# Token-major product of attention with k times v, with the norm's statistics on 8 columns, in an attention and double-MLP kernel

## The chip, the cores and the metric

The kernel runs on one core of a Trainium2 chip. The metric is the time of one execution on the device in microseconds (us). TensorE (PE in the profile; PEld is its loading of stationary operands) multiplies matrices and writes to the accumulator memory PSUM, of which a core has 8 banks of 512 columns in 32-bit floats; VectorE (DVE) and ScalarE (ACT) read and write PSUM and the on-chip memory SBUF; GpSimd (POOL) and SyncE (SP) issue transfers (DMA) to and from main memory.

## The reference

Linear attention without softmax, a root-mean-square norm, and two MLPs, all in 32-bit floats. There are 8 batches, 8 heads, 576 tokens of each batch and 64 columns of each head, so 4608 tokens and 512 columns after the heads are laid side by side; the MLPs have 2048 hidden columns.

```python
kv = einsum('bhsd,bhse->bhde', k, v)
out = einsum('bhsd,bhde->bhse', q, kv)
rms = sqrt(mean(out * out, axis=-1, keepdims=True) + 1e-06)
x = (out / rms * g_norm)            # then (batch, token) by (head, column)
h = x @ moe_w_in;   x = (moe_s * relu(h) ** 2 + moe_b) @ moe_w_out
h = x @ moe2_w_in;  x = (h * cos(h)) @ moe2_w_out
```

## The kernel before

Tokens go in 9 blocks of 512 (`TB`). The first three blocks pass the first MLP step by step, 48 steps, 16 for each block and each for one hidden tile of 128 columns (`mm_h`, lines 654 to 671, and `mm_o`, lines 704 to 730); the other six wait in main memory (`x1_d`) and pass it later in *pairs* of hidden tiles (`mm_h2`, `mm_o1`), in which seven products take the place of eight; then all tokens pass the second MLP in the same pairs. An operand of full precision is kept as two parts, a rounded one and the remainder (`fp32r`), and a product is three matmuls of such parts. Where `f32` operands are multiplied directly, a matmul appears as two instructions.

Attention is cut into *units* (`attn_unit`, line 566): one block and one pair of heads `hp`, 128 columns. There are 9 x 4 = 36 units. The units of block 0 run at the start of the kernel (`native`); those of block 1 beside the first steps, those of blocks 2 to 8 beside steps 16 to 40. A block of 512 tokens and a batch of 576 don't fit: in blocks 1 to 7 the border of two batches lies 64, 128, 192, 256, 320, 384 and 448 tokens into the block, and the block has two *segments* with a matrix kv of their own (`segments`, line 467).

A unit does this. The matrix kv of two heads is made by 64-column products (line 542) and copied into the diagonal of `kvf` (line 552). The query tile `qT`, 128 columns of two heads by 512 tokens, comes from four transpositions on TensorE in block 0 (line 579) and from a VectorE transpose of 32 x 32 blocks later (line 599). The product (line 610) has kv as the stationary operand and the tokens moving, one matmul for each segment, so the result `xps` has the heads' columns on the partitions and 512 tokens along the columns. ScalarE squares it (line 613) and, after block 0, copies it into `qT` (line 617) so that the bank comes free. The mean of squares over the 64 columns of a head, which lie on partitions, is a product with the matrix `ones` that holds 1/64 in two diagonal squares (line 619; after block 0 in two rounded parts made at lines 623 and 624, then lines 628 and 629); the result stands on every partition of the head. From it ScalarE takes the reciprocal root and its square (lines 634, 636), VectorE refines the root by one Newton step and scales the product by it and by -g (lines 638 to 643). For the first three blocks `split_x` (line 558) makes the two parts; for the others the tile is stored to `x1_d` (line 648).

The order of every engine's instructions is worked out beforehand by a planner (class `Plan`): each `op` names its engine, an assumed cost in us, a due time, what it writes and reads, and a `margin` that its readers and the next user of its buffer keep. The planner places operations by their earliest start and due time, and hands out buffers of a pool (`t`: 6 tiles of 512 columns; `qT`: 2; `qh` and `ql`: one each; the banks `a0` to `a3`, `h0` to `h3`) to whichever comes next. After block 0, attention has the banks h2 and h3 for its kv products, its products and its mean of squares. Each engine executes its list strictly in this order. Stores go through SP's queue; a buffer that is stored is free for its next writer once the store has landed. Lines 945 to 950 are 40 filler matmuls on the identity, which the planner puts where TensorE would have nothing else.

The tiles `qT`, `qh`, `ql`, `kvf`, the query and kv loads and the identity `ident` lie in a pool `early`, whose room a pool `late` takes over in the stage of the pairs.

Of the kernel before, what the change touches and what calls it, by code (L numbers as in the profile page):

```python
# [10 lines left out]
F32 = mybir.dt.float32  # L11
F32R = mybir.dt.float32r
I32 = mybir.dt.int32
U32 = mybir.dt.uint32
AF = mybir.ActivationFunctionType
ALU = mybir.AluOpType

P = 128
TB = 512
# [4 lines left out]
NE = 3  # L24
# [19 lines left out]
LATE_BY, SLIP = 2.0, 1.5  # L44
# [124 lines left out]
def fused_kernel(  # L169
# [14 lines left out]
    nc = tc.nc  # L184
    B, H, S, D = q.shape
    NT, DM = out.shape
    DFF = moe_w_in.shape[1]
    KC = DM // P
# [10 lines left out]
    EPS = 1e-6  # L199

    cpool = ctx.enter_context(tc.tile_pool(name="cpool", bufs=1))
# [15 lines left out]
    def f32(ap):  # L217
        return ap.bitcast(F32)
# [28 lines left out]
    def pref(slots):  # L247
        return Ref(slots, lambda s: psum.tile([P, TB], F32, tag=s, name=s))

    def slots(name, n, start=0):  # L250
        return [f"{name}{i}" for i in range(start, start + n)]

    WO, WI, RAW = slots("wo", NF), slots("wi", NF), ["raw"]
    T, C = slots("t", 6), slots("c", 5)
    K_RAW, V_RAW, Q_RAW = ["kv_raw"], ["raw"], ["q_raw", "q_raw1"]
    KV_F = slots("kvf", KC)
    QT, QH, QL = ["qT", "qT1"], ["qh"], ["ql"]
# [14 lines left out]
    ACC, HB0, HB1, HB2, HB3 = slots("a", 4), ["h0"], ["h1"], ["h2"], ["h3"]  # L272


    ones = cpool.tile([P, P], F32R, name="ones")
    nc.vector.memset(f32(ones), 0.0)
    for j in range(2):

        nc.vector.memset(f32(ones)[j * D:(j + 1) * D, j * D:(j + 1) * D], 1.0 / D)
    kv_f, kv_ref = {}, {}  # L280
    for n in range(KC):
        z, u = divmod(n, 2)
# [272 lines left out]

    xs = {}

    def split_x(j, c, t, by):
        x = xs[j, c] = sref(X[c], F32R, (2, TB))
        op("ACT", 0.62, by, lambda: nc.scalar.copy(x.t[:, 0], t.t), w=[x], r=[t])  # L560
        op("DVE", 0.69, by, lambda: nc.vector.tensor_tensor(
            out=x.t[:, 1], in0=t.t, in1=f32(x.t[:, 0]), op=ALU.subtract), w=[x], r=[t])

    ms_ops, x_ops = [], []

    def attn_unit(j, hp, by, after=()):

        native = j == 0
        segs = segments(j)
        for off, n, b, s in segs:  # L570
            if s == 0 and (j == 0 or hp % 2 == 0):
                kv_unit(j, b, [hp] if j == 0 else [hp, hp + 1], by - 9, after)
        qT = sref(QT + QH + QL if native else QT)
        if j == 0:
            ps = pref([ACC[0], *HB2])

            def transpose():
                for c in range(KC):
                    nc.tensor.transpose(
                        ps.t[:, c * P:(c + 1) * P], q0[hp].t[:, 0, c, :], ident  # L580
                    )

            op("PE", 0.45, by - 11, transpose, w=[ps], r=[q0[hp]])
            op("ACT", 0.48, by - 10, lambda: nc.scalar.copy(qT.t, ps.t), w=[qT], r=[ps])
        else:
            raw = sref(Q_RAW)

            def load(off, n, b, s, z):
                h, d0 = 2 * hp + z // 2, 32 * (z % 2)
                (nc.gpsimd if j > 1 and z > 5 else nc.sync).dma_start(  # L590
                    out=raw.t.rearrange("p (c d) -> p c d", d=32)[32 * z:32 * z + 32, off // 32:(off + n) // 32, :],
                    in_=q[b, h, s:s + n, d0:d0 + 32].rearrange("(c t) d -> t c d", t=32),
                )

            for seg in segs:
                for z in range(4):
                    op(*(("SUM", 1.0) if j > 1 and z > 5 else ("SP", 0.5)), by - 17, lambda seg=seg, z=z: load(*seg, z),
                       p=[raw], after=after, margin=LATE_BY)
            op("DVE", 0.6, by - 11, lambda: nc.vector.transpose(out=qT.t, in_=raw.t), w=[qT], r=[raw], margin=SLIP,
               after=x_ops[-1:])  # L600
        kvs = [kv_f[b % 2, hp // 2] for off, n, b, s in segs]
        kv_refs = [kv_ref[b % 2, hp] for off, n, b, s in segs]
        xps = pref([*ACC[1:3], *HB3] if j == 0 else HB2 + HB3)
        sq = sref(T)
        ms = pref(ACC[3:] if j == 0 else HB2 + HB3)

        def mm_x():
            for (off, n, b, s), kvt in zip(segs, kvs):
                sl = slice(off, off + n)
                nc.tensor.matmul(xps.t[:, sl], kvt.t[:, hp % 2], qT.t[:, sl], start=True, stop=True)  # L610

        x_ops.append(op("PE", 0.9, by - 8, mm_x, w=[xps], r=[qT, *kv_refs], keep=kvs))
        op("ACT", 0.48, by - 7, lambda: nc.scalar.activation(sq.t, xps.t, AF.Square), w=[sq], r=[xps])
        x = xps
        if not native:
            x = qT
            op("ACT", 0.48, by - 7, lambda: nc.scalar.copy(qT.t, xps.t), w=[qT], r=[xps], margin=SLIP)
        if native:
            op("PE", 0.9, by - 6, lambda: nc.tensor.matmul(
                ms.t, f32(ones), sq.t, start=True, stop=True), w=[ms], r=[sq])  # L620
        else:
            sqh, sql = sref(QH, F32R), sref(QL, F32R)
            op("ACT", 0.52, by - 7, lambda: nc.scalar.copy(sqh.t, sq.t), w=[sqh], r=[sq], keep=[sql], margin=SLIP / 2)
            op("DVE", 0.6, by - 6, lambda: nc.vector.tensor_tensor(
                out=sql.t, in0=sq.t, in1=f32(sqh.t), op=ALU.subtract), w=[sql], r=[sq, sqh], margin=SLIP)

            def mm_s():
                nc.tensor.matmul(ms.t, ones, sqh.t, start=True, stop=False)  # L628
                nc.tensor.matmul(ms.t, ones, sql.t, start=False, stop=True)

            ms_ops.append(op("PE", 0.45, by - 5, mm_s, w=[ms], r=[sqh, sql]))

        r0, a = sref(T), sref(T)
        op("ACT", 0.48, by - 4, lambda: nc.scalar.activation(r0.t, ms.t, AF.Abs_reciprocal_sqrt, bias=EPS),
           w=[r0], r=[ms])
        op("ACT", 0.52, by - 3, lambda: nc.scalar.activation(a.t, r0.t, AF.Square, scale=math.sqrt(0.5)),
           w=[a], r=[r0])
        op("DVE", 0.66, by - 2, lambda: nc.vector.scalar_tensor_tensor(
            out=a.t, in0=ms.t, scalar=EPS, in1=a.t, op0=ALU.add, op1=ALU.mult), w=[a], r=[ms],
           margin=SLIP if j else 0)  # L640
        op("DVE", 0.6, by - 2, lambda: nc.vector.scalar_tensor_tensor(
            out=r0.t, in0=a.t, scalar=-1.5, in1=r0.t, op0=ALU.add, op1=ALU.mult), w=[r0], r=[a])
        op("DVE", 0.66, by - 1, lambda: nc.vector.scalar_tensor_tensor(
            out=a.t, in0=x.t, scalar=g_neg, in1=r0.t, op0=ALU.mult, op1=ALU.mult), w=[a], r=[x, r0, g_ref])
        if j < NE:
            split_x(j, hp, a, by)
        else:
            op("SP", 0.8, by, lambda: nc.sync.dma_start(out=x1_d[hp][:, j * TB:(j + 1) * TB], in_=a.t),
               w=[x1_ref[j, hp]], r=[a])

# [419 lines left out]
```

## Time and profile before

| | |
|---|---|
| median of 3 runs | 1633.51 us (1630.72 to 1633.92) |
| the profiled execution | 1634.23 us |
| its span in the profile | 1632.4 us |
| its mean granted TensorE clock | 0.999 |
| instructions | 23647 |
| PE busy | 1613.6 us, 8672 matmuls |
| DVE busy | 1137.3 us, 1796 instructions |
| ACT busy | 932.4 us, 1571 instructions |
| POOL busy | 58.6 us |

The span runs from the first to the last instruction of the program, and the execution takes 1.8 us more than its span. Busy time is what an engine's own records cover. Matmuls are pipelined and the ends of one overlap the next, so a busy PE does not mean a PE at its peak. The profile names an instruction by its line, and a tile by its pool's name without the number: `t` is any of t0 to t5, `h` any of h0 to h3, and `x_d` is `x1_d` or `x2_d`.

### The profile page before, as it was taken

How to read it: one execution, taken by the hardware profiler on the slowest of the kernel's cores; microseconds unless marked ns; L12 is line 12 of the kernel's file. 1: busy time of each engine (PE TensorE's matmuls, PEld its weight loads, DVE VectorE, ACT ScalarE, POOL GpSimd, SP SyncE). 2: the span in 40 equal slices, each digit the busy share in tenths (PEclk: the TensorE clock that was granted, in tenths of full speed). 3: DMA queues.
4: the chain of work that ended last, by engine and by line, in shares of the span. 5: the costliest groups of instructions: out<-in, count | busy, mean ns of one | idle time of the engine just before them, and what ended most of it. 6: DMA issues, size and time to landing. Idle time of an engine off the chain costs nothing.

```text
span 1632.4 us, 23647 instructions
## 1 busy us (share of the span) xinstructions
PE 1613.6 (99%) x8672; PEld 1422.6 (87%) x8672; DVE 1137.3 (70%) x1796; ACT 932.4 (57%) x1571; POOL 58.6 (4%) x94
## 2 busy tenths in 40 slices
PE   8999999999999999999999999999999999999998
PEld 6678887779999999999999989989899898998997
DVE  6887887785776756767667767667667668668564
ACT  6897765555555555555556555545546546446443
POOL 1131121000000000000000000000000000000000
PEclk9999999999999999999999999999999999999999
DMA  9965688826666747757756435444444534544431
GB/s 305 262 191 129 172 204 233 215 76 203 226 207 221 250 155 245 252 181 246 245 182 228 159 121 163 154 123 144 161 133 131 172 117 137 163 128 136 148 116 46
DMA packets 202419, 288.88 MB, mean 177 GB/s; under 512 B 87744, under 2 KB 132800, under 8 KB 202304
## 3 DMA queue, kind: packets, MB, share of 16 engines
q1 hardware_dynamic: 195376, 266.40, 52.8%
q0 software_dynamic: 6400, 20.45, 4.3%
q8 instruction: 69, 1.13, 0.3%
q10 hardware_dynamic: 528, 0.52, 0.1%
q14 instruction: 46, 0.38, 0.1%
HBM read 228.59 MB, written 58.72 MB: 176 GB/s over the span
## 4 chain that ended last, share of the span: by engine, by line
PE 94%; DMA 3%; DVE 1%; ACT 1%; issue 0%; SPq 0%; DVEq 0%; ACTq 0%
PE h L862 36%; PE a L719 22%; PE a L757 11%; PE h L719 8%; PE h L757 5%; PE h L662 2%; PE h L664 2%; PE h L663 2%; PE a L711 2%; PE h L610 1%; DMA w1i_d<-t 1%; PE h L542 1%; DMA wo<-in_v_dram 1%; PE h L628 0%; DMA w2i_d<-t 0%
## 5 line engine op out<-in xcount | busy, mean ns | idle before, releaser
L862 PE MATMUL h<-shared,wi 128*128 128x384 f32 x2208 | 459.0, 337 | 2.2 <-ACT t L874 2.2
L862 PEld LDWEIGHTS h<-shared,wi 128*128 128x128 f32 x2208 | 391.3, 188 | 16.4 <-ACT t L874 2.6
L719 PE MATMUL a<-wo,wi 128*128 128x512 f32 x964 | 258.6, 391 | 0.0
L874 ACT COPY t<-h 128x384 f32<-128x384 f32 x235 | 112.3, 478 | 198.5 <-PE h L862 180.3
L719 PEld LDWEIGHTS a<-wo,wi 128*128 128x128 f32 x964 | 180.0, 188 | 33.6
L757 PE MATMUL a<-wi,wo 128*128 128x256 f32 (+1 forms) x1152 | 203.7, 317 | 0.0
L757 PEld LDWEIGHTS a<-wi,wo 128*128 128x128 f32 x1152 | 178.7, 188 | 18.0
L719 PE MATMUL h<-wo,wi 128*128 128x512 f32 x482 | 130.1, 392 | 0.0
L916 ACT ACTIVATE wi<-wi 128x768 f32<-128x768 f32 x96 | 81.4, 848 | 76.7 <-DVE wi L914 76.7
L862 PE MATMUL h<-g,wi 128*128 128x384 f32 x552 | 123.0, 337 | 0.0
L862 PE MATMUL h<-late,wi 128*128 128x384 f32 x528 | 118.6, 335 | 0.0
L719 PE MATMUL a<-g,wo 128*128 128x512 f32 x456 | 116.5, 395 | 0.0
L908 ACT ACTIVATE wi<-wi 128x768 f32<-128x768 f32 x95 | 80.5, 848 | 47.0 <-DVE wi L878 44.9
L719 PEld LDWEIGHTS h<-wo,wi 128*128 128x128 f32 x482 | 89.8, 188 | 16.0
L757 PE MATMUL h<-wi,wo 128*128 128x512 f32 x384 | 100.7, 394 | 0.8 <-DVE wi L937 0.8
L719 PEld LDWEIGHTS a<-g,wo 128*128 128x128 f32 x456 | 84.7, 188 | 18.2
L862 PEld LDWEIGHTS h<-late,wi 128*128 128x128 f32 x528 | 94.7, 188 | 5.3
L862 PEld LDWEIGHTS h<-g,wi 128*128 128x128 f32 x552 | 97.2, 188 | 2.0 <-ACT t L874 0.2
L878 DVE TENSOR_TENSOR wi<-h,t 128x384 f32<-128x384 f32 x113 | 62.8, 556 | 48.6 <-PE h L862 35.0
L912 DVE SCALAR_TENSOR_TENSOR wi<-wi,wi 128x768 f32<-128x768 f32 x95 | 90.7, 955 | 1.7
L918 DVE TENSOR_TENSOR wi<-wi,wi 128x768 f32<-128x768 f32 x95 | 90.6, 954 | 1.4
L874 ACT COPY c<-h 128x384 f32<-128x384 f32 x85 | 40.7, 479 | 88.2 <-PE h L862 88.0
(190 smaller groups left out, 2528.4 us busy)
## 6 DMA issues: line engine op xcount, KB each, us to landing
wi<-w2i_d SPq DMA_DIRECT2D x144, 512.0 KB, 4.3
wi<-w1i_d SPq DMA_DIRECT2D x96, 512.0 KB, 4.7
late<-x_d SPq DMA_DIRECT2D x36, 384.0 KB, 5.9
wo<-in_moe_w_out_dram SPq DMA_DIRECT2D x24, 512.0 KB, 6.9
w2i_d<-t SPq DMA_DIRECT2D x48, 256.0 KB, 5.4
wi<-w2i_d SPq DMA_DIRECT2D x48, 256.0 KB, 2.7
x_d<-t SPq DMA_DIRECT2D x40, 256.0 KB, 2.6
w1i_d<-t SPq DMA_DIRECT2D x32, 256.0 KB, 3.9
```

The lines of the kernel that those rows point to most:

```text
L662: nc.tensor.matmul(h.t, wh, hi, start=(c == 0), stop=False)
L663: nc.tensor.matmul(h.t, wh, lo, start=False, stop=False)
L664: nc.tensor.matmul(h.t, wl, hi, start=False, stop=(c == KC - 1))
L719: nc.tensor.matmul(o.t, a, b, start=(first and z == 0), stop=(last and z == 2))
L757: nc.tensor.matmul(dst, x[:, sl], y[:, src], start=(first and z == i == 0), stop=(last and z == 2), skip_group_check=a >= 4)
L862: nc.tensor.matmul(o.t[:, 0:HT], a, b, start=(first and c == z == 0), stop=(c == 1 and z == 2), skip_group_check=not first)
L874: op("ACT", 0.52, by + 1, lambda: nc.scalar.copy(dst(), o.t[:, 0:HT]), p=[s], r=[o])
L878: op("DVE", 0.57, by + 1, lambda: nc.vector.tensor_tensor(out=h[f].t[:, half * HT:(half + 1) * HT], in0=a.t[:, 0:HT], in1=s.t, op=ALU.add) ...
L908: op("ACT", act, by, lambda u=u, x=x: nc.scalar.activation(u.t, x.t, AF.Identity, scale=1.0 / TWO_PI, bias=0.25), w=[u], r=[x])
L912: op("DVE", one, by + 2, lambda u=u, x=x: nc.vector.scalar_tensor_tensor(out=u.t, in0=x.t, scalar=1.0 / TWO_PI, in1=u.t, op0=ALU.mult, op1 ...
L916: op("ACT", act, by + 4, lambda u=u: nc.scalar.activation(u.t, u.t, AF.Sin, scale=TWO_PI, bias=0.5 * math.pi), w=[u])
L918: op("DVE", one, by + 5, lambda u=u, x=x: nc.vector.tensor_tensor(out=u.t, in0=u.t, in1=x.t, op=ALU.mult), w=[u], r=[x])
```

## The change

The product of a unit is turned round. The 128 tokens of a chunk are now the stationary operand and kv moves, so the result has the tokens on the partitions and, for each of four chunks, 128 columns of two heads. Where the border of two batches cuts a chunk, the chunk is done in two matmuls with 64 stationary columns each. The sum of squares runs along columns (one VectorE reduction to 8 columns: 4 chunks of 2 heads), the root and its refinement work on tiles of 8 columns (`norm`), the product is scaled by it with a broadcast, and four transpositions on TensorE turn the scaled tile back to columns on the partitions, into a bank `back`. ScalarE and VectorE read it from there with the scale -g. The matrix `ones`, the copy of the product into `qT`, the two parts of the squares and the two matmuls on them go; block 0 loses its full-precision product with `ones`. The scaled tile takes `qh` or `ql` after block 0, a tile of `t` in it.

```diff
@@ -251,7 +251,7 @@
         return [f"{name}{i}" for i in range(start, start + n)]
 
     WO, WI, RAW = slots("wo", NF), slots("wi", NF), ["raw"]
-    T, C = slots("t", 6), slots("c", 5)
+    T, C, NORM = slots("t", 6), slots("c", 5), slots("n", 4)
     K_RAW, V_RAW, Q_RAW = ["kv_raw"], ["raw"], ["q_raw", "q_raw1"]
     KV_F = slots("kvf", KC)
     QT, QH, QL = ["qT", "qT1"], ["qh"], ["ql"]
@@ -272,11 +272,6 @@
     ACC, HB0, HB1, HB2, HB3 = slots("a", 4), ["h0"], ["h1"], ["h2"], ["h3"]
 
 
-    ones = cpool.tile([P, P], F32R, name="ones")
-    nc.vector.memset(f32(ones), 0.0)
-    for j in range(2):
-
-        nc.vector.memset(f32(ones)[j * D:(j + 1) * D, j * D:(j + 1) * D], 1.0 / D)
     kv_f, kv_ref = {}, {}
     for n in range(KC):
         z, u = divmod(n, 2)
@@ -555,13 +550,7 @@
 
     xs = {}
 
-    def split_x(j, c, t, by):
-        x = xs[j, c] = sref(X[c], F32R, (2, TB))
-        op("ACT", 0.62, by, lambda: nc.scalar.copy(x.t[:, 0], t.t), w=[x], r=[t])
-        op("DVE", 0.69, by, lambda: nc.vector.tensor_tensor(
-            out=x.t[:, 1], in0=t.t, in1=f32(x.t[:, 0]), op=ALU.subtract), w=[x], r=[t])
-
-    ms_ops, x_ops = [], []
+    x_ops = []
 
     def attn_unit(j, hp, by, after=()):
 
@@ -600,51 +589,54 @@
                after=x_ops[-1:])
         kvs = [kv_f[b % 2, hp // 2] for off, n, b, s in segs]
         kv_refs = [kv_ref[b % 2, hp] for off, n, b, s in segs]
-        xps = pref([*ACC[1:3], *HB3] if j == 0 else HB2 + HB3)
-        sq = sref(T)
-        ms = pref(ACC[3:] if j == 0 else HB2 + HB3)
+        xps = pref([*ACC[1:], *HB3] if j == 0 else HB2 + HB3)
+        sq, y = sref(T), sref(T if native else QH + QL)
+        norm = sref(NORM, F32, (3, 2 * KC))
+        back = pref([*ACC[1:], *HB3] if j == 0 else HB2 + HB3)
 
         def mm_x():
-            for (off, n, b, s), kvt in zip(segs, kvs):
-                sl = slice(off, off + n)
-                nc.tensor.matmul(xps.t[:, sl], kvt.t[:, hp % 2], qT.t[:, sl], start=True, stop=True)
-
-        x_ops.append(op("PE", 0.9, by - 8, mm_x, w=[xps], r=[qT, *kv_refs], keep=kvs))
-        op("ACT", 0.48, by - 7, lambda: nc.scalar.activation(sq.t, xps.t, AF.Square), w=[sq], r=[xps])
-        x = xps
-        if not native:
-            x = qT
-            op("ACT", 0.48, by - 7, lambda: nc.scalar.copy(qT.t, xps.t), w=[qT], r=[xps], margin=SLIP)
-        if native:
-            op("PE", 0.9, by - 6, lambda: nc.tensor.matmul(
-                ms.t, f32(ones), sq.t, start=True, stop=True), w=[ms], r=[sq])
+            for c in range(KC):
+                for (off, n, b, s), kvt in zip(segs, kvs):
+                    lo, hi = max(off, c * P), min(off + n, (c + 1) * P)
+                    if lo < hi:
+                        nc.tensor.matmul(xps.t[lo - c * P:hi - c * P, c * P:(c + 1) * P], qT.t[:, lo:hi],
+                                         kvt.t[:, hp % 2], start=True, stop=True)
+
+        def heads(t):
+            return t.rearrange("p (c e) -> p c e", e=D)
+
+        x_ops.append(op("PE", 0.95, by - 8, mm_x, w=[xps], r=[qT, *kv_refs], keep=kvs))
+        op("ACT", 0.6, by - 7, lambda: nc.scalar.activation(sq.t, xps.t, AF.Square), w=[sq], r=[xps])
+        op("DVE", 0.62, by - 6, lambda: nc.vector.reduce_sum(
+            out=norm.t[:, 0], in_=heads(sq.t), axis=mybir.AxisListType.X), w=[norm], r=[sq])
+        op("ACT", 0.2, by - 5, lambda: nc.scalar.activation(
+            norm.t[:, 1], norm.t[:, 0], AF.Abs_reciprocal_sqrt, scale=1.0 / D, bias=EPS), w=[norm])
+        op("ACT", 0.2, by - 5, lambda: nc.scalar.activation(
+            norm.t[:, 2], norm.t[:, 1], AF.Square, scale=math.sqrt(0.5 / D)), w=[norm])
+        op("DVE", 0.1, by - 4, lambda: nc.vector.scalar_tensor_tensor(
+            out=norm.t[:, 2], in0=norm.t[:, 0], scalar=D * EPS, in1=norm.t[:, 2], op0=ALU.add, op1=ALU.mult), w=[norm])
+        op("DVE", 0.1, by - 4, lambda: nc.vector.scalar_tensor_tensor(
+            out=norm.t[:, 1], in0=norm.t[:, 2], scalar=-1.5, in1=norm.t[:, 1], op0=ALU.add, op1=ALU.mult), w=[norm])
+        op("DVE", 0.75, by - 4, lambda: nc.vector.tensor_tensor(
+            out=heads(y.t), in0=heads(xps.t), in1=norm.t[:, 1].unsqueeze(2).to_broadcast([P, 2 * KC, D]), op=ALU.mult),
+            w=[y], r=[xps, norm], margin=SLIP if j else 0)
+
+        def turn():
+            for c in range(KC):
+                nc.tensor.transpose(back.t[:, c * P:(c + 1) * P], y.t[:, c * P:(c + 1) * P], ident)
+
+        op("PE", 0.5, by - 3, turn, w=[back], r=[y])
+        if j < NE:
+            x = xs[j, hp] = sref(X[hp], F32R, (2, TB))
+            op("ACT", 0.72, by - 1, lambda: nc.scalar.activation(x.t[:, 0], back.t, AF.Identity, scale=g_neg),
+               w=[x], r=[back, g_ref])
+            op("DVE", 0.75, by, lambda: nc.vector.scalar_tensor_tensor(
+                out=x.t[:, 1], in0=back.t, scalar=g_neg, in1=f32(x.t[:, 0]), op0=ALU.mult, op1=ALU.subtract),
+                w=[x], r=[back, g_ref])
         else:
-            sqh, sql = sref(QH, F32R), sref(QL, F32R)
-            op("ACT", 0.52, by - 7, lambda: nc.scalar.copy(sqh.t, sq.t), w=[sqh], r=[sq], keep=[sql], margin=SLIP / 2)
-            op("DVE", 0.6, by - 6, lambda: nc.vector.tensor_tensor(
-                out=sql.t, in0=sq.t, in1=f32(sqh.t), op=ALU.subtract), w=[sql], r=[sq, sqh], margin=SLIP)
-
-            def mm_s():
-                nc.tensor.matmul(ms.t, ones, sqh.t, start=True, stop=False)
-                nc.tensor.matmul(ms.t, ones, sql.t, start=False, stop=True)
-
-            ms_ops.append(op("PE", 0.45, by - 5, mm_s, w=[ms], r=[sqh, sql]))
-
-        r0, a = sref(T), sref(T)
-        op("ACT", 0.48, by - 4, lambda: nc.scalar.activation(r0.t, ms.t, AF.Abs_reciprocal_sqrt, bias=EPS),
-           w=[r0], r=[ms])
-        op("ACT", 0.52, by - 3, lambda: nc.scalar.activation(a.t, r0.t, AF.Square, scale=math.sqrt(0.5)),
-           w=[a], r=[r0])
-        op("DVE", 0.66, by - 2, lambda: nc.vector.scalar_tensor_tensor(
-            out=a.t, in0=ms.t, scalar=EPS, in1=a.t, op0=ALU.add, op1=ALU.mult), w=[a], r=[ms],
-           margin=SLIP if j else 0)
-        op("DVE", 0.6, by - 2, lambda: nc.vector.scalar_tensor_tensor(
-            out=r0.t, in0=a.t, scalar=-1.5, in1=r0.t, op0=ALU.add, op1=ALU.mult), w=[r0], r=[a])
-        op("DVE", 0.66, by - 1, lambda: nc.vector.scalar_tensor_tensor(
-            out=a.t, in0=x.t, scalar=g_neg, in1=r0.t, op0=ALU.mult, op1=ALU.mult), w=[a], r=[x, r0, g_ref])
-        if j < NE:
-            split_x(j, hp, a, by)
-        else:
+            a = sref(T)
+            op("ACT", 0.72, by - 1, lambda: nc.scalar.activation(a.t, back.t, AF.Identity, scale=g_neg),
+               w=[a], r=[back, g_ref])
             op("SP", 0.8, by, lambda: nc.sync.dma_start(out=x1_d[hp][:, j * TB:(j + 1) * TB], in_=a.t),
                w=[x1_ref[j, hp]], r=[a])
 
```

## Rows read from the trace of the kernel before

Times count from the start of the span. A form is partitions x elements and type; x and a number is how many instructions a row merges, whose time runs from the first start to the last end.

**Rows 1.** The page: busy time by engine, and the chain that ended last, by engine.

```profile
PE 1613.6 (99%) x8672; PEld 1422.6 (87%) x8672; DVE 1137.3 (70%) x1796; ACT 932.4 (57%) x1571; POOL 58.6 (4%) x94
...
PE 94%; DMA 3%; DVE 1%; ACT 1%; issue 0%; SPq 0%; DVEq 0%; ACTq 0%
```

**Rows 2.** Stretches of the span: busy us of PE, PEld, DVE, ACT, POOL; granted clock; DMA share; GB/s.

```profile
250.00:300.00 50.00, 47.87 (x309) 37.73 (x308) 35.93 (x59) 28.12 (x54) 9.64 (x14) 1.00 0.88 232
300.00:350.00 50.00, 46.93 (x232) 36.45 (x232) 39.88 (x68) 30.26 (x58) 0.00 (x0) 1.00 0.61 157
1200.00:1600.00 400.00, 400.00 (x1998) 361.34 (x1997) 269.16 (x402) 210.13 (x331) 0.00 (x0) 1.00 0.43 137
```

**Rows 3.** Waits of PE between 60 and 420 us: total us, times, longest.

```profile
PE h L610 <- DVE qT L599: 3.3, 2, 1.8
PE h L628 <- ACT qT L617: 1.2, 1, 1.2
PE h L542 <- ACT qT L617: 0.7, 1, 0.7
```

**Rows 4.** Chain of waits from 262 to 310 us: start, us, what.

```profile
261.81 0.87 PE h L610 x4
...
275.89 5.12 DMA x_d<-t
...
291.89 5.78 DMA w1i_d<-t
```

**Rows 5.** Timeline of DVE, 329 to 352 us: start, us, engine, line, operation, out<-in, form.

```profile
329.19 0.75 DVE L643 SCALAR_TENSOR_TENSOR t<-qT,small,t 128x512 f32<-128x512 f32 x1
...
330.32 0.71 DVE L599 STREAM_TRANSPOSE qT<-q_raw 128x512 f32<-128x512 f32 x1
...
345.87 0.71 DVE L599 STREAM_TRANSPOSE qT<-q_raw 128x512 f32<-128x512 f32 x1
```

**Rows 6.** Timeline of PE, 20 to 36 us; in brackets the idle time before and its releaser.

```profile
22.88 0.60 PE L579 MATMUL h<-ident,wi 128*128 128x128 f32 x4
23.32 0.39 PE L949 MATMUL h<-ident 128*128 128x128 f32 x2
...
29.77 2.17 PE L949 MATMUL h<-ident 128*128 128x128 f32 x18
32.37 0.49 PE L662 MATMUL h<-shared,wi 128*128 128x512 f32 x1 [0.42 <-ACT shared L560]
33.34 0.50 PE L663 MATMUL h<-shared,wi 128*128 128x512 f32 x1 [0.48 <-DVE shared L561]
```

**Rows 7.** Timeline of PE, 68.5 to 71.2 us, around a product of k and v.

```profile
68.77 0.40 PE L664 MATMUL h<-shared,wi 128*128 128x512 f32 x1
69.10 0.69 PE L542 MATMUL h<-raw,kv_raw 128*64 128x64 f32 x16
...
70.19 0.29 PE L542 MATMUL h<-tails 128*64 128x64 f32 x4
70.41 0.50 PE L662 MATMUL h<-shared,wi 128*128 128x512 f32 x1
```

**Rows 8.** Timeline of PE, 112.2 to 113 us.

```profile
112.60 0.39 PE L629 MATMUL h<-ql,ones 128*128 128x512 f32 x1
112.83 0.40 PE L662 MATMUL h<-shared,wi 128*128 128x512 f32 x1
```

**Rows 9.** Groups by line: busy us, mean ns of one, idle us before and its releasers.

```profile
L354 DVE TENSOR_SCALAR c<-c 128x512 f32<-128x512 f32 x64 | 27.1, 428 | 34.3 <-ACT c L353 33.9
...
L643 DVE SCALAR_TENSOR_TENSOR t<-qT,small,t 128x512 f32<-128x512 f32 x32 | 23.9, 747 | 0.3
...
L599 DVE STREAM_TRANSPOSE qT<-q_raw 128x512 f32<-128x512 f32 x32 | 22.6, 706 | 0.4
...
L617 ACT COPY qT<-h 128x512 f32<-128x512 f32 x32 | 18.7, 583 | 0.0
```

**Rows 10.** Timeline of DVE, 11.0 to 11.4 us.

```profile
11.16 0.15 DVE L298 TENSOR_SCALAR small<-small 128x1 f32<-128x1 f32 x1
```

## The prediction

> **What bounds the kernel now.** I read the page first, for which engine fills the span, then the stretches, then TensorE's waits, then the chain through the one stretch where TensorE waits most, and last single stretches of the timeline for prices. TensorE is busy 99% of the span and 94% of the chain that ended last is its own work [rows 1]. VectorE and ScalarE stand at 70 and 57%, but a mean hides stages, so the stretches come next. From 1200 to 1600 us, where the pairs run and the change has no instruction, TensorE is busy without a break; from 250 to 350 us, in the attention stage, it is idle for 2.13 + 3.07 = 5.2 us [rows 2]. Its granted clock is 1.00 in all three, so no term below is a matter of the clock. The waits of the attention stage name all of that idle time: two for the transposed query tile, two for what ScalarE makes out of the product, 5.2 us in total [rows 3]. The chain shows what stood behind them: 5.12 us for a store of a normalised tile to land, 5.78 us for a store of weight sums [rows 4]. Both stores read a buffer of the pool t, so the next writer of it stands in front of everything queued behind it on VectorE or ScalarE. So a shorter list of VectorE and ScalarE work is worth little by itself here: what counts is TensorE's own columns, those 5.2 us, and the start of the kernel.
>
> A second thing limits how early a unit of attention can run: the query transpose starts 0.38 us after the last read of the tile of two units before has ended (329.19 + 0.75 = 329.94, then 330.32) [rows 5]. There are two such tiles, and each is held from its transpose to the last step of its unit.
>
> At the start TensorE runs filler matmuls on the identity: 18 of them in 2.17 us, then it waits 0.42 us for the rounded part and 0.48 us for the remainder of the third unit's tile [rows 6].
>
> **The change part by part.** A unit is one pair of heads for one block of 512 tokens: 36 units, of which 4 (block 0) at the start and 32 later.
>
> *The product.* Before, one unit of two segments took 0.87 us [rows 4]. After, each chunk of 128 tokens is a stationary operand of its own, with 128 moving columns and two instructions. The nearest rows are the filler matmuls, of the same shape with a weight load each: 18 take 2.17 us and 2 take 0.39 us, so one costs (2.17 - 0.39) / 16 = 0.111 us [rows 6]. Eight cost 0.89 us: +0.02 for the 16 units of blocks 2, 4, 6 and 8, whose batch border lies on a chunk's border, +0.3 us in all.
>
> In blocks 1, 3, 5 and 7 the border (64, 192, 320 or 448 tokens in) cuts a chunk into two halves of 64 tokens, so 64 stationary columns. The only rows of that form are the products of k and v. The last full matmul in front ends at 69.17, the 40 narrow ones at 70.48 [rows 7]. From the end of the first 16 (69.79) the other 24 take 0.69 us, 0.029 each, two side by side. Forty would take 1.15 us, they take 1.31: 0.16 us to get in. The full matmul behind them ends at 70.91, 0.43 us later, where two of its kind lie 0.23 us apart [rows 8]: 0.20 us to get out. So a cut chunk costs 0.16 + 0.20 and, if its halves run side by side as those do, 0.22 us. The unit: 3 x 0.22 + 0.22 + 0.36 = 1.25 us, +0.38, and for 16 units **+6.1 us**. The upper bound has the halves one after the other (0.22 more each, +9.6 us). The lower has no surplus (+0.3 us), if what those rows show comes from 64 moving columns being too few to cover a weight load, for here 128 move. I take the row's surplus whole: it is the only row of this form.
>
> The Trainium skill, TensorEngine Tiling (Array Packing), section Tiling Modes, says that a change of the tiling mode, not merely of the tile, drains the TensorE. By that rule the cut chunk pays in and out whatever its moving columns, +6.1 us; by the other reading of the row it pays nothing, +0.3. No row of the kernel before has 64 stationary columns with 128 moving ones.
>
> *The mean of squares.* Two rounded matmuls with the matrix of ones go, 2 x 0.23 = 0.46 us [rows 8]; four transpositions come. Those of the query tiles at the start are the nearest: four in 0.60 us where two filler matmuls take 0.39, so no more than 0.111 apart [rows 6], 0.44 us. -0.02 x 32 = -0.6 us. **TensorE's columns together: 0.3 + 6.1 - 0.6 = +5.8 us**, all on the path, as TensorE has next to no idle time there.
>
> *VectorE and ScalarE.* A later unit loses a subtraction and three scalar-tensor steps of about 0.7 each and gets the sum along columns (between 0.43 and 0.71, two one-input steps on as many columns; I take 0.6, as nothing says which of them it is nearer to), two steps on 8 columns at about 0.15 each, what a step on one column takes, and one product at 0.75 [rows 9, 10]: about 1.1 us less. ScalarE gives up five passes of about 0.58 [rows 9] for two, with two on 8 columns: about 1.3 us less. This is hidden behind TensorE and worth nothing directly. What it brings are buffers: a unit asks for two places of t where it asked for three, and its query tile is free after the product. So the next writer of t comes later after the store has been issued, and the query transpose no longer waits for the end of a unit [rows 5]. The wait then ends last elsewhere: at the two accumulator banks h2 and h3, which kv products, token products and transposed tiles share. I give back two thirds of the 5.2 us, **-3.5 us** (none to all of them).
>
> *The start.* The units of block 0 lose a matmul pair of full precision and get the transpositions: on the third unit's way to its tile, which ends TensorE's wait, 0.4 us less on TensorE, about 0.4 on VectorE, 0.7 on ScalarE: **-1.5 us**, between 0 (if the weight conversions take the place) and -3.1 (all of 2.17 + 0.42 + 0.48).
>
> *At nothing:* three fills of the ones matrix and four small tiles; and the identity, which now stays in use to the last unit: its room goes to the late pool, whose first load waits anyway for every tile of the early pool, which the last transpositions read. The planner, which books 0.95 us for the new product where a cut unit needs 1.25, gets another order; what it hides is TensorE's queue of main products, and if that cover is gone, its price is the third rival's.
>
> **Sum.** +5.8 - 3.5 - 1.5 = +0.8 us. The profiled execution took 1634.2 us (span 1632.4) and would take 1635.0; it stands 0.7 above the median of the runs, 1633.5, so the forecast is **1634.3 us**. A measurement of this kernel can tell about 0.2%, 3.3 us, from no change.
>
> **The rivals.**
> 1. *A cut chunk costs no surplus* (the lower bound above). Columns: 0.3 + 0.3 - 0.6 = 0; with the two gains -5.0 us, 1628.5: faster. For it: 64-column operands that move on a full array are nowhere slow. Against it: every block of kv products pays the same in and out. 16%.
> 2. *The landing stores hold as before.* The late stores of weight sums are untouched, and it was one of them that cost 5.78 us [rows 4]; with units that run sooner, query loads and these stores meet more closely. Then nothing is given back: 5.8 - 1.5 = +4.3 us, 1637.8: slower. 17%.
> 3. *The two banks become the wait.* A bank is now held from the token product over squares, sum, two small steps on each engine and the scaling, where before two copies freed it; and TensorE takes its work in order, so a bank that comes back late stops the main products queued behind the transpositions. The four waits of 5.2 us would become eight: 5.8 - 1.5 + 5.2 = +9.5 us, 1643.0: slower. It decides once both banks are held when the planner has a product due. Raw hold times (0.9 to 1.3, 0.6, 0.6, 0.7 and 0.75, then 0.4 and 0.75, and about 1 for half of a kv product and its copies) add up to under 7 us of the 15.6 that two banks give in a unit's 7.8 (two units follow in 345.87 - 330.32) [rows 5], hence 17%.
>
> **How the numbers follow.** The forecast has 47%; 3% are left for the halves one after the other (+3.5 us more). The forecast's own range is 1631 to 1638. To hold eight in ten it goes down to the first rival and past the second, without the third: 1628.5 to 1640. Faster by over 0.2%: the first rival and the forecast's edge, 19%. Slower: the second, the third and the other edge, 37%. Between: 44%.
>
> **What would show it.** In the changed profile TensorE should have 8672 + 264 = 8936 matmuls; a full chunk should take 0.22 us, a cut one about 0.58 with the entry and exit, and the main matmul behind it should end about 0.43 us after it. The query transpose should start well before the end of the unit two before. TensorE's waits between 250 and 350 us should fall from 5.2 us to 2 or less, with none named after a bank (by a step that reads h). The third unit's tile should end the filler 1.5 us earlier. The forecast is wrong if cut and whole units take the same time, or if the waits grow, or if the pairs behind 380 us change by more than a microsecond or two of waits for the stores of their own weights.

## The result: slower by 0.7%, outside the range

The changed kernel takes 1646.3 us (median of 4 runs, 1645.1 to 1646.9) where the kernel before takes 1633.7 on the same chip: a ratio of 1.0073, 95% interval 1.006 to 1.0087. In what follows a run's distance to the kernel before is its ratio to runs of that kernel on its own chip, times 1633.5 us; for the changed kernel that is **+11.9 us**. Forecast were +0.8, with a range that ended at 1640.

The page of the changed kernel, with the busy times and the chain that ended last (for [rows 1]):

```profile
span 1645.2 us, 24123 instructions
...
PE 1628.1 (99%) x8936; PEld 1436.4 (87%) x8936; DVE 1103.3 (67%) x1797; ACT 892.9 (54%) x1531; POOL 57.9 (4%) x94
...
PE 90%; DMA 5%; SPq 2%; DVE 1%; ACT 1%; issue 1%; DVEq 0%; ACTq 0%
```

TensorE still fills the span, with the 8936 matmuls that were expected; VectorE lost 34 us and ScalarE 40, and nothing of it shows in the time. TensorE's own busy time grew by 14.5 us. The columns added account for 5.3 of them (0.3 + 5.6 - 0.6, priced below), so the stretches come next (for [rows 2]; busy us of PE, PEld, DVE, ACT, POOL, then granted clock, DMA share, GB/s):

```profile
250.00:300.00 50.00, 48.56 (x358) 39.70 (x356) 30.73 (x60) 22.45 (x50) 9.63 (x14) 1.00 0.88 234
300.00:350.00 50.00, 46.28 (x276) 37.84 (x275) 35.38 (x73) 24.27 (x53) 0.00 (x0) 1.00 0.69 192
...
1200.00:1600.00 400.00, 400.00 (x1984) 358.98 (x1983) 270.97 (x403) 210.43 (x329) 0.00 (x0) 1.00 0.43 138
```

Two things are to be seen. In the attention stage TensorE idles 1.44 + 3.72 = 5.2 us, as before: nothing was given back. And from 1200 to 1600 us, where the change has no instruction, TensorE is busy all the time at the full granted clock and yet gets through 1984 matmuls where it got through 1998. That count is only a hint, as the same stretch of time holds a slightly different piece of the program (from 800 to 1200 us both kernels have 2070). But PE's busy time grew by 9 us more than the added columns explain, and the groups by line say that the same matmuls have become slower (busy us, mean ns of one; of the kernel before, then of the changed one; a 391 that becomes 395 is a duration, of which two neighbours overlap):

```profile
L719 PE MATMUL a<-wo,wi 128*128 128x512 f32 x964 | 258.6, 391 | 0.0
L719 PE MATMUL h<-wo,wi 128*128 128x512 f32 x482 | 130.1, 392 | 0.0
L757 PE MATMUL a<-wi,wo 128*128 128x256 f32 (+1 forms) x1152 | 203.7, 317 | 0.0
L719 PE MATMUL a<-g,wo 128*128 128x512 f32 x456 | 116.5, 395 | 0.0
```

```profile
L711 PE MATMUL a<-wo,wi 128*128 128x512 f32 x964 | 261.8, 395 | 0.0
L711 PE MATMUL h<-wo,wi 128*128 128x512 f32 x482 | 131.3, 394 | 0.0
L749 PE MATMUL a<-wi,wo 128*128 128x256 f32 (+1 forms) x1152 | 204.9, 318 | 0.0
L711 PE MATMUL a<-g,wo 128*128 128x512 f32 x456 | 119.3, 400 | 0.0
```

These four groups, the same count of the same forms, took 8.4 us more. From the end of one rounded matmul of 512 columns to the end of the next, both traces worked out over some 3500 of them: 229.4 ns before, 232.1 after. This is called the pace below. Matmuls of 384 columns, the largest group of all, did not slow down:

```profile
L862 PE MATMUL h<-shared,wi 128*128 128x384 f32 x2208 | 459.0, 337 | 2.2 <-ACT t L874 2.2
```

```profile
L854 PE MATMUL h<-shared,wi 128*128 128x384 f32 x2208 | 458.8, 337 | 1.8 <-ACT t L866 1.8
```

The waits of TensorE between 60 and 420 us (for [rows 3]; total us, times, longest), and the start (for [rows 6]; in brackets the idle time before):

```profile
PE h L626 <- DVE qh L620: 2.3, 1, 2.3
PE h L537 <- DMA raw<-in_v_dram: 1.3, 2, 0.7
PE h L537 <- ACT t L638: 1.1, 1, 1.1
PE h L602 <- ACT t L638: 0.4, 1, 0.4
```

```profile
31.04 0.50 PE L655 MATMUL h<-shared,wi 128*128 128x512 f32 x1 [0.29 <-DVE shared L633]
```

The waits make 5.1 us where they made 5.2, under new names: the transpositions (L626), products of k and v that wait for a bank which ScalarE's pass over the turned tile (L638) has to give back, and for v itself. The last wait of the start ends at 31.04 where it ended at 33.34, 2.3 us earlier.

Between 268 and 322 us the chain of waits now runs through query loads and the queue that issues them (for [rows 4]; start, us, what):

```profile
268.16 6.63 DMA q_raw<-in_q_dram
...
275.72 6.51 DMA q_raw<-in_q_dram
...
282.67 6.17 DMA w1i_d<-t
...
291.98 0.64 SPq L579
```

### The profile page after: what moved, and what is told of

It reads as the page before. It is cut to its first block, busy times and chain, and to the rows that moved or that the text cites. A ratio compares the mean times of both kernels' runs of the same rounds, so it can differ in the third digit from the quotient of the medians.

```text
span 1645.2 us, 24123 instructions
## 1 busy us (share of the span) xinstructions
PE 1628.1 (99%) x8936; PEld 1436.4 (87%) x8936; DVE 1103.3 (67%) x1797; ACT 892.9 (54%) x1531; POOL 57.9 (4%) x94
## 4 chain that ended last, share of the span: by engine, by line
PE 90%; DMA 5%; SPq 2%; DVE 1%; ACT 1%; issue 1%; DVEq 0%; ACTq 0%
PE h L854 35%; PE a L711 21%; PE a L749 10%; PE h L711 8%; PE h L749 5%; PE h L654 2%; PE h L655 2%; PE h L656 2%; PE a L703 2%; DMA q_raw<-in_q_dram 2%; PE h L602 1%; PE h L537 1%; SPq L579 1%; PE h L626 1%; DMA w2i_d<-t 1%
## 5 line engine op out<-in xcount | busy, mean ns | idle before, releaser
L908 ACT ACTIVATE wi<-wi 128x768 f32<-128x768 f32 x96 | 81.3, 847 | 76.9 <-DVE wi L906 76.8
```

Source lines behind the costliest of these rows:

```text
L908: op("ACT", act, by + 4, lambda u=u: nc.scalar.activation(u.t, u.t, AF.Sin, scale=TWO_PI, bias=0.5 * math.pi), w=[u])
```

## The experiments

What differs where the change has no instruction is where tiles lie. The compiled programs give every tile an address. Before, all large tiles lay at 160 modulo 512 bytes (the remainder of the address after division by 512). In the changed kernel the matrix of ones is gone from the front and four tiles of 96 bytes, made when first used, lie between the large ones, which so come to lie at 160, 256, 352, 448 or 32.

### The four small tiles in one

```diff
+    norms = cpool.tile([P, P], F32, name="norms")
...
+            if s in NORM:
+                at = NORM.index(s) * 32
+                return norms[:, at:at + math.prod(shape)].rearrange("p (a b) -> p a b", a=shape[0])
```

> The changed kernel with one edit: its four small tiles of 96 bytes lie inside one tile of 512 bytes at the place where the matrix of ones lay, so every large tile has its address of before modulo 512 again; every engine's list of instructions is that of the changed kernel. Theory A (place): a main product of 512 columns took 229.4 ns before and 232.1 ns after, 3511 of them, so 9.5 us come back: about 1637 us. Theory B (order): the slower pace comes from the planner's new order and what runs beside TensorE: about 1646 us, pace 232 ns.

Ratio 1.0025 (1.0016 to 1.0034), +4.1 us, against +11.9; the instruction lists of all engines are those of the changed kernel. The pace is 229.3 ns again. Of the groups the first is back at 258.6, the last half-way, at 117.9. The first is the one to go by: with the tiles aligned it stands at 258.5 or 258.6 in every run from here on, while the last, which moves with the order too, lies anywhere between 116.5 and 118.9:

```profile
L715 PE MATMUL a<-wo,wi 128*128 128x512 f32 x964 | 258.6, 392 | 0.0
...
L715 PE MATMUL a<-g,wo 128*128 128x512 f32 x456 | 117.9, 397 | 0.0
```

So 7.8 of the 11.9 us are the place of the tiles; 2.7 ns on each of 3511 matmuls would make 9.5, and the two intervals leave about 2.5 us either way. Its waits between 60 and 420 us, which later runs are held against, are 5.6 us:

```profile
PE h L541 <- ACT t L642: 3.5, 2, 3.2
PE h L541 <- DMA raw<-in_v_dram: 1.6, 1, 1.6
PE h L630 <- DVE qh L624: 0.5, 1, 0.5
```

### The kernel before with such gaps

```diff
+            if s in ("wi13", "wi3", "c4") and s not in shifted:
+                shifted.append(s)
+                pads.append(sb.tile([P, 24], F32, tag="n" + s, name="n" + s))
```

> The kernel before with one edit: three unused tiles of 96 bytes are put between the large tiles, where the changed kernel has its small ones (a fourth does not fit); its instructions are those of before in the same order. Theory A (place): most of the 9.5 us appear here, 1639 to 1643 us, and the pace of 512 columns rises from 229.4 to about 232 ns. Theory B (order): 1633.7 us as before, pace 229.4 ns.

Ratio 1.005 (1.0038 to 1.0063), +8.2 us, at a pace of 231.8 ns; three unused tiles of 96 bytes do to the kernel before what the change did to it:

```profile
L724 PE MATMUL a<-wo,wi 128*128 128x512 f32 x964 | 261.6, 395 | 0.0
...
L724 PE MATMUL a<-g,wo 128*128 128x512 f32 x456 | 118.1, 399 | 0.0
```

### All tiles moved, and one gap of 256 bytes

```diff
+    shift = cpool.tile([P, 8], F32, name="shift")
```

> Edit against the kernel before: one unused tile of 32 bytes in front of all the large tiles, so that every one of them moves by 32 bytes and all still lie at one and the same address modulo 512. Theory R (what counts is where the tiles of one matmul lie to each other): the rounded matmul of 512 columns stays at 229.4 ns and the time within 1.5 us of the kernel before. Theory M (what counts is the address itself, or that a small tile is there): 231 to 232.5 ns, and 5 to 10 us slower.

```diff
-            if s in ("wi13", "wi3", "c4") and s not in shifted:
+            if s in ("wi3",) and s not in shifted:
...
-                pads.append(sb.tile([P, 24], F32, tag="n" + s, name="n" + s))
+                pads.append(sb.tile([P, 64], F32, tag="n" + s, name="n" + s))
```

> The kernel before with one unused tile of 256 bytes, so that the tiles behind it, about half of the weights and the activations g, lie 256 bytes off the others modulo 512 and at the same place modulo 256. Theory 512: these mixed matmuls go at 231 to 232.5 ns, the mean between 230.3 and 231.8, and the time is 3 to 8 us longer than before. Theory 256 (only the place modulo 256 or less counts): 229.4 ns and within 1.5 us of the kernel before.

All moved: ratio 0.9999 (0.9989 to 1.0008), 229.3 ns. One gap of 256: 1.0007 (0.9996 to 1.0017), 229.4 ns, and the groups stand as in the kernel before:

```profile
L724 PE MATMUL a<-wo,wi 128*128 128x512 f32 x964 | 258.6, 391 | 0.0
...
L724 PE MATMUL a<-g,wo 128*128 128x512 f32 x456 | 116.5, 395 | 0.0
```

Neither the address itself nor a gap costs anything, and my theory of 512 bytes falls: tiles that lie 256 apart modulo 512 are as good as aligned ones. What is left is the distance modulo 256.

### No cut chunks

```diff
-                    lo, hi = max(off, c * P), min(off + n, (c + 1) * P)
-                    if lo < hi:
+                    lo, hi = c * P, (c + 1) * P
+                    if max(off, lo) < min(off + n, hi) and off <= lo:
```

> As e1, and a cut chunk is done by one matmul of 128 stationary columns with the first segment's kv; the kv of the second batch is left out for 64 tokens in each of blocks 1, 3, 5 and 7. Theory A (a change between 128 and 64 stationary columns costs 0.20 us each way): the trace of the change shows 0.37 us for a cut chunk and 0.195 us for what follows, against 0.22 us for a whole one, so 16 x 0.34 = 5.5 us less than e1. Theory B (the surplus is taken up by other idle time of TensorE): within 1.5 us of e1.

Ratio 1.0004 (0.9994 to 1.0014), +0.7 us: 3.4 us less than with the cuts, give or take some 2, where 5.5 were expected and the rival said none. The waits explain part of the rest: 7.1 us instead of 5.6. The changed kernel's own timeline has the price without them. A cut unit (10 matmuls) between two rounded ones, and a whole one (8):

```profile
194.11 0.39 PE L656 MATMUL h<-shared,wi 128*128 128x512 f32 x1
194.34 1.39 PE L602 MATMUL h<-kvf,qT 128*128 128x128 f32 x10
195.49 0.48 PE L654 MATMUL h<-shared,wi 128*128 128x512 f32 x1
...
150.20 1.56 PE L711 MATMUL a<-g,wo 128*128 128x512 f32 x6
151.60 1.05 PE L602 MATMUL h<-kvf,qT 128*128 128x128 f32 x8
```

From the end of the matmul in front (194.11 + 0.39 = 194.50) to the end of the one behind (195.97), less that one's own 0.23, a cut unit takes 1.24 us. The whole one ends 0.89 us after what is in front (151.76 to 152.65). The cut costs 0.35 us a unit, 5.6 us for sixteen. The units picked are typical: of the 16 of either kind, the 15 that have no wait in them and a matmul of 512 columns behind lie between 1.23 and 1.24 us, and between 0.89 and 0.90. The two halves of a cut chunk start 6 or 7 ns apart, so they do run side by side and the prediction's upper bound is out.

### Why nothing was given back: six runs on the waits

All but one stand against the run with the four small tiles in one (+4.1 us, waits of 5.6).

The query tile held to the end of its unit, as before the change:

```diff
-            w=[y], r=[xps, norm], margin=SLIP if j else 0)
+            w=[y], r=[xps, norm], keep=[qT], margin=SLIP if j else 0)
```

> As e1, and the query tile is kept until the scaled tile is written, close to where the kernel before let it go, so queries are loaded later again. Theory A (the early query loads crowd SP's queue and delay the stores that free tiles of t): TensorE's waits between 250 and 350 us fall from 5.1 us to 2 us or less, and the time by about 3 us against e1. Theory B (the stores of weight sums are late by themselves): the waits stay at 4 to 6 us and the time within 1.5 us of e1.

Ratio 1.0034 (1.0023 to 1.0045), +5.6 us, waits 4.5: theory B. The early release of the query tile, and the earlier loads that follow from it, are not the gain that I had booked, and no loss that stands out of the noise.

The scaled tile off t:

```diff
-        sq, y = sref(T), sref(T if native else QH + QL)
+        sq, y = sref(T), sref(T)
...
-            a = sref(T)
+            a = sref(QH + QL)
```

> Edit against the run with the four small tiles in one: the buffers of two tiles are exchanged. The scaled tile y, read at once by the transpositions, takes a place of t; the finished tile a, which is held until its store to memory has landed, takes qh or ql. Theory L (the waits that stayed are stores landing out of t): TensorE's waits between 60 and 420 us fall from 5.6 us to 3 or less, the store of the finished tile leaves the chain of waits, and the time falls by 2 to 3 us, from 1637.9 to about 1635.5. Theory B (the two banks are the wait, whatever the stores do): waits stay between 5 and 6.5 us and the time within 1 us of 1637.9.

Ratio 1.0053 (1.0035 to 1.0072), +8.7 us: slower, which neither theory had. Its six runs lie between 1636.8 and 1647.6, and the profile is of the shortest, with waits of 4.6 us, the longest one (2.3) behind the same pass of ScalarE, now for a place of ql. The wait moves along with the tile; what lengthens the other runs the profile does not show.

The landing of stores told to the planner:

```diff
-            op("SP", 0.8, by, store, p=[ref], r=[part])
+            op("SP", 0.8, by, store, p=[ref], r=[part], margin=3.5)
...
-               w=[x1_ref[j, hp]], r=[a])
+               w=[x1_ref[j, hp]], r=[a], margin=3.5)
```

> Edit against the run with the four small tiles in one: the planner, which counts a stored tile as free 2 us after its store, counts it free 5.5 us after (the landing that the chain shows), for the finished tiles and the weight sums; nothing else is edited. Theory L (TensorE's waits of 5.6 us between 60 and 420 us come from VectorE and ScalarE standing in front of a buffer whose store has not landed, with work queued behind them): the stores leave the chain, the waits fall to 3 us or less, and the time falls from about 3.6 to about 1 us over the kernel before. Theory D (data is late there whatever the order is, as the DMA engines are busy nine tenths of the stretch): waits of 5 to 8 us, named after loads instead, and the time stays within 1.5 us of that run or grows.

Ratio 1.0023 (1.0013 to 1.0032), +3.8 us, waits of 5.1 (3.0 of them before the transpositions, 2.1 for v): the time that theory D had, with its names only in part. With the same edit on the kernel before with the new block 0:

> The kernel before with the change in block 0 alone, and the longer landing of stores in the planner. If theory L holds: 2 to 4 us less than without that landing, so 4 to 6 us less than the kernel before. If theory D holds: 1 to 3.5 us less than the kernel before, as without it.

Ratio 1.0047 (1.003 to 1.0064), +7.7 us: slower than either theory had it. New waits of 2.6 us come up at L908, behind the attention stage:

```profile
PE h L908 <- ACT t L920: 2.6, 3, 1.4
```

So the other order that the planner makes has its own price. The profile is of the shortest of six runs (1637.7 to 1645.6 us); what the others lose it does not show. The gain that theory L promised came in neither run. But the edit holds for the weight sums of the later stages too, for the loads that read them as for the buffers, so this shows that telling the planner of the landing does not help, and not that the landing is no part of the wait.

Cut units booked in full:

```diff
-        x_ops.append(op("PE", 0.95, by - 8, mm_x, w=[xps], r=[qT, *kv_refs], keep=kvs))
+        x_ops.append(op("PE", 1.3 if j % 2 else 0.95, by - 8, mm_x, w=[xps], r=[qT, *kv_refs], keep=kvs))
```

> Edit against the run with the four small tiles in one: the planner books 1.3 us for the product of a unit with a cut chunk, as it takes, where it booked 0.95. If what the planner hid was worth nothing, as the prediction took it: the time within 1 us of that run (about 3.6 us over the kernel before) and waits of 4.5 to 6.5 us. If the wrong booking is why the waits were not given back: waits of 3.5 us or less and 2 to 3 us less time.

Ratio 1.0027 (1.0015 to 1.004), +4.4 us, waits of 5.1. The booking is worth nothing.

Half the query loads:

```diff
-            raw = sref(Q_RAW)
+            if hp % 2 == 0:
+                raws[j] = sref(Q_RAW)
+            raw = raws[j]
...
-            for seg in segs:
+            for seg in segs if hp % 2 == 0 else []:
```

> Edit against the run with the four small tiles in one: in blocks 1 to 8 the query tile of the first of two units is used for both, so half of the query loads are left out (and the second unit's own queries with them). Theory D (the DMA engines and their queue are what is late between 250 and 350 us): TensorE's waits between 60 and 420 us fall from 5.6 us to 3 or less, and the time by 2 to 5 us. Theory B (the handing over of banks and of places of t alone): the waits stay at 4.5 to 6.5 us and the time within 1.5 us.

Ratio 0.999 (0.998 to 1), -1.6 us: 5.7 us less than with all loads, a little over the 2 to 5 expected. One wait is left, and the stretch of 250 to 350 us loses 0.7 us instead of 5.6 (waits, then stretches; the last fence has the stretches with all query loads):

```profile
PE h L541 <- DMA raw<-in_v_dram: 0.7, 1, 0.7
```

```profile
250.00:300.00 50.00, 49.34 (x395) 40.83 (x394) 34.23 (x70) 25.18 (x57) 9.42 (x14) 1.00 0.92 264
300.00:350.00 50.00, 50.00 (x260) 41.73 (x260) 32.33 (x65) 23.26 (x49) 0.00 (x0) 1.00 0.37 111
```

```profile
250.00:300.00 50.00, 47.61 (x353) 39.17 (x352) 31.80 (x64) 22.37 (x50) 9.64 (x14) 1.00 0.89 225
300.00:350.00 50.00, 46.75 (x273) 39.16 (x272) 32.91 (x68) 24.30 (x53) 0.00 (x0) 0.97 0.69 193
```

The DMA view of 250 to 325 us, with all query loads and with half of them, each with the stores of weight sums (count, KB each, median us from issue to landing):

```profile
DMA packets 29475, 17.27 MB, mean 230 GB/s; under 512 B 22595, under 2 KB 25667, under 8 KB 29468
...
w1i_d<-t SPq DMA_DIRECT2D x10, 256.0 KB, 4.4
```

```profile
DMA packets 19058, 17.02 MB, mean 227 GB/s; under 512 B 11580, under 2 KB 14970, under 8 KB 19050
...
w1i_d<-t SPq DMA_DIRECT2D x11, 256.0 KB, 3.6
```

Nearly the same bytes went through in that time, with half the small packets: other transfers took the room and were done sooner (a DMA share of 0.37 from 300 to 350 us, where it was 0.69). The stores landed sooner too, 3.6 us for 4.4. With all query loads, late stores do stand in the chain of waits:

```profile
289.71 5.70 DMA x_d<-t
...
295.43 5.86 DMA w1i_d<-t
```

The second of them ends at 301.29 and, through four passes of ScalarE and VectorE, releases at 304.49 the longest of TensorE's waits. With half the loads the chain of the same stretch has no store in it at all. So what TensorE waits for in this stage is transfers, and it is the query loads, in strips of 32 columns or 128 bytes, that keep them back. Four edits of buffers and order leave that as it is. The planner's order differs in this run as well, and whether the packets or the instructions that issue them are the dearer half was not taken apart.

### The new way in block 0 alone

The kernel before, with the changed unit for block 0 (three small tiles in one of 288 bytes in front of the large ones) and the old one behind it:

```diff
+        if native:
+            return block0_unit(hp, by, qT, kvs, kv_refs, xps)
```

> The kernel before, with the change in the four units of block 0 alone (three small tiles in one tile of 288 bytes in front of the large ones, which move together). Theory S (the 2.3 us that the start gained is kept to the end, as nothing behind it is changed): 229.4 ns for 512 columns and 2.3 us faster than the kernel before, about 1630.1, between 1629 and 1631.5. Rival: the waits for landing stores between 250 and 350 us take it back, as they depend on when weights and queries are loaded and not on when TensorE began: within 1 us of the kernel before.

Ratio 0.9986 (0.9977 to 0.9995), -2.3 us (between 0.8 and 3.8 by the interval), which is what the start gained in the changed kernel. The gain is kept to the end, and this version beats both kernels.

## Why the prediction was wrong

**The step that failed** is "At nothing: three fills of the ones matrix and four small tiles". I costed the small tiles as instructions, which they hardly are, and not as bytes between other tiles. They cost 7.8 us of the 11.9, on the rounded matmuls of 512 columns, most of which run in stages that the change does not touch. The text itself named this as a sign of failure, a change behind 380 us, but gave it no rival and no chance.

Point by point:

- *Columns.* 8936 matmuls, as predicted. A whole unit 0.89 us (predicted 0.89), a cut unit 1.24 (1.25), four transpositions 0.44 (0.44). The first rival, no surplus for the cut, is out: 0.35 us for entry and exit with 128 moving columns, and 3.4 us less time without cuts. The Trainium skill, TensorEngine Tiling (Array Packing), section Tiling Modes, says that a change of the tiling mode drains TensorE; the trace agrees in so far as a cut unit pays 0.35 us, though a drain as such it does not show.
- *The start.* 2.3 us were gained for 1.5 predicted, within the bounds of 0 and 3.1.
- *"I give back two thirds of the 5.2 us"* failed too: nothing came back (5.1 us after; 5.6 with the tiles aligned). The second rival had this right, and its time, 1637.8, is that of the run with the small tiles in one (1633.5 + 4.1 = 1637.6). Its reason was right in part: stores do land late there and meet the query loads. But it blamed units that run sooner, and holding the query tile back changed nothing; half the query loads took the waits away. I had read the chain's 5 us for a landing as something that buffers decide, where the DMA share of 0.88 in the same stretch [rows 2] hinted at what the landing waited for.
- *The third rival* has the names right and the size not: products do wait for a bank that a pass over a turned tile gives back, but in place of the old waits and not on top of them.
- *VectorE and ScalarE* gave up 34 and 40 us and it was worth nothing, as predicted.

The sum as it came out: +0.3 whole chunks, +5.6 cuts, -0.6 transpositions, -2.3 start and +7.8 place give +10.8; the other 1.1 us were not separated and are less than the intervals leave open.

## What to carry to other kernels

Before costing a small new tile at nothing, look where the allocator puts it: here tiles of 96 bytes shifted the tiles behind them against those in front, and that cost more than all the rest of the change, where a gap of 256 bytes cost nothing. Small tiles go into one tile ahead of the large ones. Where a wait's chain ends in a DMA, look at the DMA share of that stretch, and at what else is in flight, before booking a gain for a buffer that comes free sooner. And where a change gains in one stage and loses in another, try it in the first alone.

## What the runs showed of the hardware

**The place of operands.** A rounded matmul of 512 columns goes at a pace that depends on how its moving tile lies to the stationary tiles, above all to the one that is loaded next while it runs. Where the two addresses are equal modulo 256 bytes, the pace is 229.3 ns in the kernel before (3406 matmuls) and in the one with a gap of 256 (3406, of which 1929 lie 256 apart). Where they are not, it is 232.5 in the changed kernel (2511) and 232.4 in the kernel before with gaps of 96 (2589); matmuls there that do lie so, among neighbours that don't, take 230.7 and 230.0 (852 and 888). That is some 3 ns, 1.4%. Distances of 32, 64, 96, 128, 160, 192 and 224 bytes, where a run has over a hundred cases of one, all cost it: from 231.2 (64) to 233.3 (96). Groups of 20 to 30 scatter more. Where the moving tile lies like its own stationary tile but not like the next, the pace is 233.0 in the changed kernel (227) and 232.3 with gaps of 96 (225); the other way round it is 231.9 (161) and 231.4 (169), so the next one counts more, and not alone. Matmuls of 384 columns show none of this: 175.0 ns in the changed kernel where neither lies like it (2026), 175.0 in the kernel before (2825). What in the chip makes it was not shown.

The Trainium skill, SBUF — State Buffer, section "A bandwidth-pool intuition that's wrong", gives TensorE a second, independent read port for the weight load. From that one would expect no load to slow a matmul by where its moving tile lies. The runs here do show 3 ns; whether it is the load that makes them they do not show.

**The clock after a wait.** In the run with the four small tiles in one, TensorE idled 3.25 us between 300 and 305 us, and the granted clock of the next 5 us was 0.71 (columns as in the stretches above):

```profile
300.00:305.00 5.00, 1.75 (x16) 1.19 (x16) 2.60 (x6) 2.31 (x5) 0.00 (x0) 0.95 0.83 238
305.00:310.00 5.00, 5.00 (x50) 4.49 (x47) 0.00 (x0) 1.21 (x3) 0.00 (x0) 0.71 0.55 126
```

Between levels of 1.2 and 2.4 GHz that is 2.9 of 5 us at the lower one, 1.5 us of work lost on top of the wait. The changed kernel's profile, with its waits spread over several places, shows 1.00 in this stage.
